# Batch 0's q turned once per pair, factors in the bank of the product of values, a fourth buffer of split P, and a new table of order

## The chip, the cores and the metric

The kernel runs on one core of a Trainium2 chip. The metric is the device time of one execution in microseconds (us); lower is better. An execution is timed as a whole; a profiled execution gives a trace of every instruction on the engines: TensorE (PE, matmuls; PEld its weight loads), VectorE (DVE), ScalarE (ACT), GpSimd (POOL) and SyncE (SP, which issues the DMAs).

## What is computed

Soft-capped attention over 4 batches, 12 heads, 448 positions and 64 columns per head, followed by two matrix products with a leaky relu between them. All inputs are fp32; cut to what matters:

```python
scores = q @ k.T / sqrt(64)                 # (4, 12, 448, 448)
scores = cap * tanh(scores / cap)           # cap = 30
attn   = softmax(scores, axis=-1)
x      = (attn @ v) -> (1792, 768)          # heads side by side
h      = x @ w_in                           # (768, 2048)
g      = max(h, 0) + alpha * min(h, 0)      # alpha per column
out    = g @ w_out                          # (2048, 768)
```

## The kernel before

Every step is put into one list, `Plan`, with a priority, the planner's guess of its time on each engine that may do it, and what it reads and writes. `order()` then plays the list through once on the host side, engine by engine, and the resulting order of each engine's queue is what the chip runs; nothing is reordered later. The guesses are constants at the head of the file: times of loads on SP (`load`, `load_w`, `LOAD_C`), `SWITCH` for a change of PE's tiling, `SAME` (how far down in priority PE may look for a step in the tiling that it is in), `PEN`, `PEN2` and `PENP` (what a step must gain before it goes to DVE or POOL). `OFF` adds a number to the priority of each group of steps. Where the plan has nothing ready for PE in the early part, it puts in fills: matmuls of the identity that compute nothing that is used (line 1236), one after another into a free bank.

PSUM is divided in two score tiles of two banks each (`s`) and four single banks (`p`). A step that needs a `p` bank takes a handle; of the kind that the attention uses at most three are out at once.

The work comes in three kinds. Attention goes by units, one pair of heads each. Batch 0 is done in exact fp32 in two parts, columns 0 to 192 of all six pairs (part 0), then 192 to 448 (part 1): `attention32` turns k (in part 0 only) and q by matmuls with the identity (`turn`, line 546; two fp32 matmuls for each of four chunks of 112 rows) and an eviction; then come scores (line 582), tanh, row maxima (line 623), exponentials (line 630), turns of P (line 734), and in `PV_32` the factors (1 over the row sums, spread along the columns by matmuls with the identity, line 796) and the product of values (line 807). The turned q of one part lies in one of two small buffers in `qkTs`, so each pair's q is turned once for each part: the chunks that the part touches, 2 of 4 in part 0 (4 matmuls) and 3 of 4 in part 1 (6 matmuls). The factors take a bank of their own and are evicted to `xs` first; then the product takes a second bank, and `xout_32` multiplies it with the factors on DVE and splits the result into two f16 halves in `xring`. Batch 1 has exact scores, and its first two units use `PV_32` as well, with all 448 columns. The other units use f16 pairs (high and low half): `split` makes them, P passes through one of `PW` buffers `pws` and is turned by a DMA (`ptall<-pw`).

The weights come as 64-bit words of which DVE makes fp32 (three steps, lines 1061, 1065 and 1071), and each is scaled and split into two f16 halves. The product with w_in (line 965) is evicted through the leaky relu (line 975) into `gall`; the product with w_out (line 1006) is evicted in halves of 384 columns (line 435) and stored by SP (line 1029).

In the program's names a digit behind a tile is a buffer: `wp6` and `wp7` hold the raw q of batch 0 (pairs 0 to 2 and 3 to 5), `wp4` and `wp5` its raw k, `wp0` to `wp3` the words of w_in; `rvs`, `nat`, `xring` and `vs16` take v of batch 0. `gall`, `tall` and `ptall` are lent to batch 0 for scores, turned k and turned P.

Of the kernel before, what the change touches and what calls it, by code (L numbers as in the profile page):

```python
# [31 lines left out]
B0_P = 174.12
LD_P = -270.26
LO_P = 908.9
MM_P = 2448.92
X_P = 475.19
ST_P = 63.05
ST1_P = -43.26
PV_P = 390.15
QK_P = -78.75  # L40
V_P = 196.4
WI_P = 21.53
WI_S = -63.55
A_S = 5.03
MM1_P = 480.9
WO_P = -182.63
WO_S = 86.83
WT_P = -1018.45
WT_S = 131.8
B1_P = 701.09  # L50
B_S = 239.81
EVAC_P = -930.96
# [13 lines left out]
PW = 3  # L66
QA = 0
# [5 lines left out]
SAME = 209.56  # L73
LOAD_C = (600, 1400, 950)
# [205 lines left out]
def kernel(  # L280
# [1003 lines left out]
```

## Time and profile before

| | |
|---|---|
| time, median of 3 runs | 671.75 us (669.79 to 672.01) |
| profiled execution, own time | 671.53 us |
| its span | 669.7 us |
| PE busy | 652.8 us (97%) |
| DVE busy | 466.5 us (70%) |
| ACT busy | 419.8 us (63%) |
| POOL busy | 264.1 us (39%) |
| chain that ended last | PE 78%, DVE 9%, ACT 6%, DMA 5% |

The busy time of an engine is summed over the whole span; a stretch in which two engines take turns, and one in which PE alone never stops, look alike in it. So the table is to be read with the row of tenths for each engine (40 slices of 16.7 us) and with tables by stretch. The first 140 us hold batch 0's and the start of batch 1's attention and the conversion of the weights; the last 400 hold mostly the two products.

### The profile page before, as it was taken

Reading aid. Unit: us, or ns where it says so; the run is one execution under the profiler, and the core shown is the slowest. Engines: PE = TensorE matmul, PEld = TensorE weight load, DVE = VectorE, ACT = ScalarE, POOL = GpSimd, SP = SyncE. Lnnn points to the kernel's source line nnn. Section 1 sums busy time; section 2 is a strip of 40 time slices with the busy share of each in tenths; the row PEclk is TensorE's granted clock in tenths of the full one; section 3 lists DMA queues with packets and bytes.
Section 4 is the critical chain, followed back from the end, with each engine's and each line's share of the span. In section 5 each row is a group of like instructions: output and inputs, shape, how many; then the busy total and the mean of one; then the engine's idle time right before and its main releaser. Section 6 shows DMA issues by size and latency. Waiting matters only on the chain.

```text
span 669.7 us, 13360 instructions
## 1 busy us (share of the span) xinstructions
PE 652.8 (97%) x5042; PEld 409.5 (61%) x5042; DVE 466.5 (70%) x887; ACT 419.8 (63%) x865; POOL 264.1 (39%) x393
## 2 busy tenths in 40 slices
PE   9999999799999999999999999999999999999997
PEld 8877777678877565554555555545555555556664
DVE  3799999999999858888887778889983104440000
ACT  2868999889789867778666567767783113331000
POOL 1224556257776724577664344556540000000000
PEclk9999999999999999999999999999999999999999
DMA  9998573954844499976939899686645300000111
GB/s 237 267 269 262 165 203 95 257 157 108 182 80 102 80 178 191 180 138 115 163 73 197 167 201 208 124 166 127 122 89 102 73 25 0 1 1 0 37 35 23
DMA packets 190048, 87.06 MB, mean 130 GB/s; under 512 B 156256, under 2 KB 186272, under 8 KB 189984
## 3 DMA queue, kind: packets, MB, share of 16 engines
q1 hardware_dynamic: 189840, 86.22, 59.6%
q8 instruction: 39, 0.64, 0.4%
q14 instruction: 25, 0.20, 0.1%
q10 hardware_dynamic: 144, 0.00, 0.0%
HBM read 45.82 MB, written 5.51 MB: 77 GB/s over the span
## 4 chain that ended last, share of the span: by engine, by line
PE 78%; DVE 9%; ACT 6%; DMA 5%; issue 2%; POOL 0%; ACTq 0%; SPq 0%; DVEq 0%; POOLq 0%
PE p L1006 29%; PE p L965 26%; PE p L780 5%; DMA ptall<-pw 4%; PE s L588 4%; PE s L582 3%; PE p L807 3%; PE p L1236 2%; PE p L734 2%; DVE mxs L623 2%; PE p L546 2%; ACT tall L630 1%; DVE wp L1065 1%; DVE wp L1071 1%; DMA rvs<-in_v_dram 1%
## 5 line engine op out<-in xcount | busy, mean ns | idle before, releaser
L965 PE MATMUL p<-xring,wi 128*128 128x448 f16 (+2 forms) x1440 | 225.0, 315 | 0.8 <-DVE vam L398 0.7
L1006 PE MATMUL p<-wp,gall 128*128 128x384 f16 x1344 | 223.3, 326 | 0.0
L965 PEld LDWEIGHTS <-wi 128*128 128x128 f16 x1440 | 135.2, 98 | 85.6 <-issue 6.1
L1006 PEld LDWEIGHTS <-gall 128*128 128x128 f16 x1344 | 129.7, 98 | 89.0 <-issue 5.3
L630 ACT ACTIVATE tall<-tall,mxs 128x448 f32<-128x448 f32 x126 | 82.8, 659 | 19.9 <-POOL mxs L625 9.7
L975 DVE SCALAR_TENSOR_TENSOR gr<-p,ca_g,gr 128x448 f32<-128x448 f32 (+2 forms) x80 | 46.8, 586 | 50.9 <-ACT gr L435 50.2
L623 DVE TENSOR_REDUCE mxs<-tall 128x2 f32<-128x896 f32 x63 | 67.6, 1079 | 8.5 <-ACT tall L619 7.9
L625 POOL TENSOR_SCALAR mxs<-mxs,small 128x2 f32<-128x2 f32 x59 | 30.5, 517 | 68.7 <-DVE mxs L623 56.1
L442 POOL TENSOR_TENSOR pw<-tall,pw 128x448 f16<-128x448 f32 x41 | 46.4, 1133 | 18.8 <-ACT pw L429 13.2
L435 ACT ACTIVATE wp<-p,small 128x384 f32<-128x384 f32 x22 | 12.7, 577 | 63.5 <-PE p L1006 63.5
L435 ACT ACTIVATE gr<-p,cs_g 128x448 f32<-128x448 f32 (+2 forms) x55 | 30.3, 550 | 30.5 <-PE p L965 30.1
L649 POOL TENSOR_SCALAR rr<-sums 128x2 f32<-128x2 f32 (+2 forms) x70 | 22.6, 323 | 65.6 <-ACT tall L630 49.2
L619 ACT ACTIVATE tall<-s,ams 128x896 f32<-128x896 f32 x42 | 41.5, 997 | 6.9 <-DVE pw L442 2.5
L429 ACT ACTIVATE pw<-tall 128x448 f16<-128x448 f32 x51 | 28.9, 571 | 24.6 <-DMA ptall<-pw 22.0
L429 ACT ACTIVATE gall<-gr 128x384 f16<-128x384 f32 (+4 forms) x60 | 27.4, 463 | 23.3 <-DVE gr L975 23.1
L780 PE MATMUL p<-ptall,vs 112*64 112x448 f16 x384 | 40.5, 355 | 0.6 <-DMA ptall<-pw 0.6
L442 DVE TENSOR_TENSOR pw<-tall,pw 128x448 f16<-128x448 f32 x43 | 29.8, 692 | 14.0 <-ACT pw L429 12.0
L442 DVE TENSOR_TENSOR gall<-gr,gall 128x64 f16<-128x64 f32 (+4 forms) x66 | 32.9, 499 | 6.2 <-ACT gall L429 3.2
L442 POOL TENSOR_TENSOR gall<-gr,gall 128x256 f16<-128x256 f32 (+4 forms) x46 | 34.0, 742 | 5.6 <-ACT gall L429 3.5
L780 PEld LDWEIGHTS <-vs 112*64 112x64 f16 x384 | 21.0, 110 | 18.6 <-issue 5.4
L435 ACT ACTIVATE tall<-tall,rr 128x448 f32<-128x448 f32 x42 | 27.0, 660 | 8.3 <-DVE rr L652 7.3
L588 PE MATMUL s<-qkTs 64*128 64x448 f16 (+1 forms) x288 | 28.3, 352 | 0.7 <-ACT tall L619 0.7
(175 smaller groups left out, 976.9 us busy)
## 6 DMA issues: line engine op xcount, KB each, us to landing
wp<-in_moe_w_in_dram SPq DMA_DIRECT2D x16, 768.0 KB, 7.7
wp<-in_moe_w_out_dram SPq DMA_DIRECT2D x16, 768.0 KB, 5.9
rvs<-in_v_dram SPq DMA_DIRECT2D x38, 224.0 KB, 3.3
rqk<-in_q_dram SPq DMA_DIRECT2D x12, 224.0 KB, 3.0
rqk<-in_k_dram SPq DMA_DIRECT2D x12, 224.0 KB, 3.5
ptall<-pw SPq DMA_TRANSPOSE x128, 3.2
wp<-in_q_dram SPq DMA_DIRECT2D x6, 224.0 KB, 7.3
wp<-in_k_dram SPq DMA_DIRECT2D x6, 224.0 KB, 9.3
```

Of the source, the lines that this page charges most:

```text
L429: nc.scalar.activation(out=o, in_=i, func=AF.Copy)
L435: nc.scalar.activation(out=o, in_=i, func=AF.Copy, scale=s)
L442: (nc.gpsimd if e == "pool" else nc.vector).tensor_tensor(out=o, in0=a, in1=b, op=ALU.subtract)
L588: yield lambda z=z, w=w: nc.tensor.matmul(s[rows, x, :S], q[a, z * S + cols.start:z * S + cols.stop], q[a, w * S:(w + 1) * S], start=(z == ...
L619: op(pr, {"act": (152 if reg else 245) + 377 * 2}, lambda e: nc.scalar.activation(out=t, in_=s[:, :, :S].rearrange("p c (j k) -> p c j k", ...
L623: op(pr, {"dve": 136 + 469 * 2}, lambda e: nc.vector.tensor_reduce(out=mt, in_=t, axis=AX.XY, op=ALU.max), r=tr, w=[mr], port=False)
L625: op(pr, {"dve": 200, "pool": 265}, lambda e: (nc.gpsimd if e == "pool" else nc.vector).tensor_scalar(out=mt, in0=mt, scalar1=ncap, scalar ...
L630: nc.scalar.activation(out=t[:, x], in_=t[:, x], func=AF.Exp, scale=capr, bias=mt[:, x:x + 1], accum_out=sums[:, u.idx % 3, col + x:col + ...
L780: nc.tensor.matmul(pv[x * D:(x + 1) * D, :n], vs[:, z, c:c + D], u.pt[x][:CP, y * NCH + kc], start=(i == 0), stop=(i == len(prods) - 1))
L965: nc.tensor.matmul(ps_p[h.slot][:, :n], w[:, z, kk, :], x[:, d, o:o + n], start=(kk == 0 and z == d), stop=(kk == NPAIR - 1 and z == 1))
L975: op(pr, {"dve": 198 + 1.07 * n}, lambda e: nc.vector.scalar_tensor_tensor(out=t, in0=ps_p[h.slot][:, :n], scalar=ca_g[:, j:j + 1], in1=t, ...
L1006: nc.tensor.matmul(ps_p[h.slot][:, :NH], g[j][:, d, t * P:(t + 1) * P], w[:, z, hf * NH:(hf + 1) * NH], start=(j == 0 and z == d), stop=(j ...
```

## The change

Six things are changed. (1) The planner's constants and its table `OFF` are others, and the loads' times in the plan are shorter (w_in 3400 to 2350, w_out 2500 to 1950, q, k and v 1000 to 880 ns), which moves instructions on all engines. (2) Batch 0's q is turned once per pair, all four chunks in part 0, and the turned q is kept in the place of the raw one (`qT`, in `wp6` and `wp7`). (3) `PV_32` takes one bank instead of two: the product of values goes to columns 0 to n, then the factors to columns n to 2n of the same bank; `xout_32` evicts the factors, then multiplies. Since 2n must fit in 512 columns, batch 1's two units do 256 and 192 columns apart. (4) `PW` is 4 instead of 3. (5) `QA` is 1 instead of 0: the q and k of batches 2 and 3 are split by a scaling to f16 and two subtractions of 256 columns on DVE, instead of a scaling in fp32, a copy and a subtraction. (6) The very last eviction is cut in two halves of 192 columns, one on ACT and one on DVE, and the last store's second DMA is issued on ACT's queue.

The diff, with the two tables `OFF` (212 numbers each) and most of the constants left out:

```diff
-PEN = 11684.16
-PEN2 = -1614.45
-PENP = 10077.68
+PEN = 24324.02
+PEN2 = 429.82
+PENP = 13233.71
...
-PW = 3
-QA = 0
+PW = 4
+QA = 1.0
-SAME = 209.56
-LOAD_C = (600, 1400, 950)
+SAME = 531.89
+LOAD_C = (600, 1400, 800)
...
     qkTs = ct([P, 3, NQK, CP], F16, "qkTs")
-    aux = qkTs[:, 2].rearrange("p g t -> p (g t)").bitcast(F32)
-    qzs = [aux[:, i * 256:(i + 1) * 256] for i in range(2)]
-    qzr = [(("qkT", 2), i * 256, (i + 1) * 256) for i in range(2)]
     ident, identr = ct([P, P], F32, "ident"), ("ident", 0, 1)
     ones = ct([NF, P], BF16, "ones")
     mxt = ct([NF, 128], F32, "mxt")
-    xs = ct([P, 2, 2, 256], F32, "xs")
-    diags = xs.rearrange("p a b n -> p (a b n)").rearrange("p (i n) -> p i n", n=P)
-    xsf = xs.rearrange("p a b n -> p (a b n)")
+    xs = ct([P, 2, 256], F32, "xs")
     vs16 = ct([P, 2, 2, 2 * NCH * D], F16, "vs16")
...
     def load(prio, dst, src, b, pair, w):
-        op(prio, {"sp": (600, 1400, 1000)}, lambda e: nc.sync.dma_start(out=dst.rearrange("p (h c) -> p h c", h=2),
+        op(prio, {"sp": (600, 1400, 880)}, lambda e: nc.sync.dma_start(out=dst.rearrange("p (h c) -> p h c", h=2),
                                                           in_=heads(src, b, pair)), w=w)
     class Unit:
         pass
-    raw32, v0 = {}, {}
+    raw32, qT, v0 = {}, {}, {}
...
                 raw32[i, pair] = t, (("wp", i + pair // 3), o, o + n)
+                qT[pair] = wpair[i + pair // 3].rearrange("p a b -> p (a b)")[:, o:o + S]
                 plan.tag = 155 + 2 * pair + (i == 6)
...
-    def xs_parts(u, n):
-        o = 512 * (u.idx % 2) if n <= 256 else 0
-        return [(xsf[:, a:a + n], ("xs", a, a + n)) for a in (o, o + (256 if n <= 256 else 512))]
-
-    def PV_32(u, prio, n, vt, vr):
-        (R, rt), _ = xs_parts(u, n)
+    xs_no = [0]
+
+    def PV_32(u, prio, a, n, vt, vr):
+
         h = plan.handle("a")
-        def rows_of(e):
-            for i, c, y, rows, cols in u.facts:
-                nc.tensor.matmul(ps_p[h.slot][y * D:(y + 1) * D, cols], rr[:, i, c:c + 1].to_broadcast([P, D]), ident[:, rows], start=True, stop=True)
-
-        op(prio, {"pe": n / 0.6 + 65}, rows_of, r=[(("r", i), c, c + 1) for i, c, *_ in u.facts] + [identr], w=[h], mode=1)
-        op(prio, either(n, True, f=True), lambda e: scaled(e, R, ps_p[h.slot][:, :n], vb[u.b].s), r=[h, (vb[u.b].tok, 7, 9)], w=[rt], port=False)
-        g_ = plan.handle("a")
-
         def PV(e):
-            pv = ps_p[g_.slot]
+            ps = ps_p[h.slot]
             for kc in range(NCH):
                 for y in range(2):
                     c = (y * NCH + kc) * D
-                    nc.tensor.matmul(pv[y * D:(y + 1) * D, :n], vt[:, c:c + D], u.pv[y][:, kc],
+                    nc.tensor.matmul(ps[y * D:(y + 1) * D, :n], vt[:, c:c + D], u.pv[y][:, kc, a:a + n],
                                      start=(kc == 0), stop=(kc == NCH - 1))
-
-        op(prio, {"pe": 4 * (n / 0.6 + 20)}, PV, r=[("pt", z, z + 3 * u.js + n) for z in u.po] + [vr], w=[g_], rows=0.875, mode=1)
-        return g_
+            for i, c, y, rows, cols in u.facts:
+                if a <= cols.start < a + n:
+                    nc.tensor.matmul(ps[y * D:(y + 1) * D, n + cols.start - a:n + cols.stop - a], rr[:, i, c:c + 1].to_broadcast([P, D]),
+                                     ident[:, rows], start=True, stop=True)
+
+        op(prio, {"pe": 4 * (n / 0.6 + 20) + n / 0.6 + 65}, PV, w=[h], rows=0.9, mode=1,
+           r=[(("r", i), c, c + 1) for i, c, *_ in u.facts] + [identr, vr] + [("pt", z + a, z + a + 3 * u.js + n) for z in u.po])
+        return h
     def xout_32(u, prio, h, n, o):
-        x, ((R, rt), (t, tt)) = xring[:, xslot(u.b, u.pair)], xs_parts(u, n)
+        x = xring[:, xslot(u.b, u.pair)]
+        i = xs_no[0] % 2
+        xs_no[0] += 1
+        t, tt = xs[:, i, :n], ("xs", i, i + 1)
         hi, lo = x[:, 0, o:o + n], x[:, 1, o:o + n]
-        op(prio, {"dve": 160 + 1.04 * n}, lambda e: nc.vector.tensor_tensor(out=t, in0=ps_p[h.slot][:, :n], in1=R, op=ALU.mult),
-           r=[h, rt], w=[tt], port=False)
+        op(prio, either(n, True, f=True), lambda e: scaled(e, t, ps_p[h.slot][:, n:2 * n], vb[u.b].s), r=[h, (vb[u.b].tok, 7, 9)], w=[tt], port=False)
+        op(prio, {"dve": 160 + 1.04 * n}, lambda e: nc.vector.tensor_tensor(out=t, in0=ps_p[h.slot][:, :n], in1=t, op=ALU.mult),
+           r=[h], w=[tt], port=False)
         op(prio, either(n, pool=True), lambda e: copy(e, hi, t), r=[tt], w=[xr(u.b, u.pair, 0, o, n)])
...
             op(prio, either(S, True), lambda e, h=h: copy(e, kt[:, pair, :], ps_p[h.slot][:, :S]), r=[h], w=[ktr], port=False)
-        h = plan.handle("a")
         rq, rqr = raw32[6, pair]
-        c0 = o // CP
-        nch = -(-(o + n) // CP) - c0
-        qi = u.idx % 2
-        u.q, qr = qzs[qi][:, :n], (qzr[qi][0], qzr[qi][1], qzr[qi][1] + n)
-        op(prio, {"pe": 60 + 205 * nch}, lambda e, h=h: turn(h, rq, c0, nch), r=[rqr, identr], w=[h, qr], rows=0.7, mode=1)
-        op(prio, either(n, True), lambda e, h=h: copy(e, u.q, ps_p[h.slot][:, o - c0 * CP:o - c0 * CP + n]), r=[h], w=[qr], port=False)
-        u.k, u.qk, u.scores, u.scale, u.joint, u.dma = kt[:, pair], [qr, ktr], scores_32, [icap], [icap], False
+        if part == 0:
+            h = plan.handle("a")
+            op(prio, {"pe": 60 + 205 * NCH}, lambda e, h=h: turn(h, rq, 0, NCH), r=[rqr, identr], w=[h], rows=0.7, mode=1)
+            op(prio, either(S, True), lambda e, h=h: copy(e, qT[pair], ps_p[h.slot][:, :S]), r=[h], w=[rqr], port=False)
+        u.q = qT[pair][:, o:o + n]
+        u.k, u.qk, u.scores, u.scale, u.joint, u.dma = kt[:, pair], [rqr, ktr], scores_32, [icap], [icap], False
         po = u.idx % 2 * 8 * n
...
         def finish(u):
-            h = PV_32(u, u.prio + X_P, n, *v0[0, u.pair])
+            h = PV_32(u, u.prio + X_P, 0, n, *v0[0, u.pair])
             xout_32(u, u.prio + X_P, h, n, o)
...
         else:
-            h = PV_32(u, u.prio + PV_P, S, *u.v)
-            xout_32(u, u.prio + PV_P, h, S, 0)
+            for a, n in ((0, 2 * P), (2 * P, S - 2 * P)):
+                h = PV_32(u, u.prio + PV_P, a, n, *u.v)
+                xout_32(u, u.prio + PV_P, h, n, a)
...
         osc = vb[b].osc if t < 3 else joint[:, b // 2:b // 2 + 1]
-        op(EVAC_P + prio * 1e-4, either(NH, True, f=True), lambda e: scaled(e, osb[:, cols], ps_p[h.slot][:, :NH], osc),
-           r=[h, *oscs], w=[osr], port=False)
         last = b == B - 1 and t == 3
+        cut = 2 if last and hf else 1
+        for i in range(cut):
+            z = slice(i * NH // cut, (i + 1) * NH // cut)
+            times = {("act", "dve")[i]: either(NH // 2, True, f=True)[("act", "dve")[i]]} if cut > 1 else either(NH, True, f=True)
+            op(EVAC_P + prio * 1e-4, times, lambda e, z=z: scaled(e, osb[:, cols][:, z], ps_p[h.slot][:, z], osc),
+               r=[h, *oscs], w=[(osr[0], osr[1] + z.start, osr[1] + z.stop)], port=False)
         if hf == 0 and not last:
...
             for t0, m, dst in rows:
-                op(EVAC_P, {"sp": (550, 1000, 800)}, lambda e, p=p, m=m, dst=dst: nc.sync.dma_start(
+                queue = {"act": 60} if cut > 1 and p else {"sp": (550, 1000, 800)}
+                op(EVAC_P, queue, lambda e, p=p, m=m, dst=dst: (nc.scalar if e == "act" else nc.sync).dma_start(
                     out=dst[:, a], in_=osb[p:p + m, a]), r=[osr])
...
             t = flat
-        op(prio, {"sp": (550, 1800, (3400 if split else 2500) if wide else 1700)}, lambda e: nc.sync.dma_start(
+        op(prio, {"sp": (550, 1800, (2350 if split else 1950) if wide else 1700)}, lambda e: nc.sync.dma_start(
             out=t.rearrange("p (c f) -> p c f", c=DM // P) if split else t, in_=src), w=[(("wp", i), 0, 2 * DM)] if wide else [fr])
```

Where instructions stand in the two programs is shown at two places. On SP, the first loads of the program, before; `in_q`, `in_k` and `in_v` are 224 KB for one pair, `in_moe_w_in` is a chunk of 768 KB:

```order
L462 DMA wp6_99<-in_q_dram 112x2x256
L462 DMA wp4_97<-in_k_dram 112x2x256 x2
L1049 DMA wp0_93<-in_moe_w_in_dram 128x6x256
L462 DMA wp6_99<-in_q_dram 112x2x256
L462 DMA wp7_100<-in_q_dram 112x2x256
L1049 DMA wp2_95<-in_moe_w_in_dram 128x6x256
L462 DMA rvs_111<-in_v_dram 112x2x256 x2
L462 DMA wp4_97<-in_k_dram 112x2x256
```

and after, where the same lines have the numbers 457 and 1047:

```order
L457 DMA wp6_99<-in_q_dram 112x2x256
L457 DMA wp4_97<-in_k_dram 112x2x256 x2
L1047 DMA wp0_93<-in_moe_w_in_dram 128x6x256
L457 DMA wp6_99<-in_q_dram 112x2x256
L457 DMA wp7_100<-in_q_dram 112x2x256
L457 DMA wp5_98<-in_k_dram 112x2x256
L457 DMA nat_113<-in_v_dram 112x2x256
L457 DMA xring_109<-in_v_dram 112x2x256
L457 DMA wp4_97<-in_k_dram 112x2x256
L1047 DMA wp2_95<-in_moe_w_in_dram 128x6x256
```

Up to the fifth load nothing moves; then two loads of k and two of v stand ahead of the second chunk of w_in, which was sixth.

On PE, the first products of values of batch 0's part 0 (line 807 before, 792 after) with the factors (796 in both) around them, before; line 415 and 418 are the two halves of a maximum over partitions, line 734 is a turn of P:

```order
L796 MATMUL p_64<-ident,rr 64x128 x2
L796 MATMUL p_64<-ident,rr 64x64 x2
L415 MATMUL p_63<-ident,n_wi 4x128
L807 MATMUL p_65<-ptall,rvs 64x192 x8
L418 LDWEIGHTS ones
L418 MATMUL p_63<-mxt,ones 128x4
L796 MATMUL p_64<-ident,rr 64x128 x2
L796 MATMUL p_64<-ident,rr 64x64 x2
L734 MATMUL p_65<-ident,gall 112x128 x4
```

and after, where line 410 and 413 are that maximum and line 542 is a turn of q (`wp_100` is the raw q of pairs 3 to 5):

```order
L542 MATMUL p_63<-ident,wp_100 64x112 x8
L410 MATMUL p_65<-ident,n_wi 4x128
L792 MATMUL p_66<-ptall,rvs 64x192 x8
L796 MATMUL p_66<-ident,rr 64x128 x2
L796 MATMUL p_66<-ident,rr 64x64 x2
L413 LDWEIGHTS ones
L413 MATMUL p_65<-mxt,ones 128x4
L542 MATMUL p_63<-ident,wp_100 64x112 x8
```

The factors, which stood in a bank of their own (`p_64`) on both sides of other work, follow the product of values in its bank (`p_66`), and whole turns of q (8 matmuls) stand beside them.

## Rows read from the trace of the kernel before

**Rows 1.** The page, parts 1 and 2: busy time, and tenths of 40 slices

```profile
PE 652.8 (97%) x5042; PEld 409.5 (61%) x5042; DVE 466.5 (70%) x887; ACT 419.8 (63%) x865; POOL 264.1 (39%) x393
...
PE   9999999799999999999999999999999999999997
...
DVE  3799999999999858888887778889983104440000
```

**Rows 2.** Four stretches: length, then busy PE, PEld, DVE, ACT, POOL, clock, DMA

```profile
0.00:20.00 20.00, 18.55 (x258) 16.64 (x258) 8.38 (x15) 8.16 (x16) 3.54 (x13) 1.00 0.96 247
20.00:140.00 120.00, 110.47 (x1199) 86.85 (x1196) 114.89 (x209) 104.75 (x237) 48.23 (x73) 1.00 0.74 207
140.00:265.00 125.00, 123.60 (x1050) 90.13 (x1048) 108.72 (x201) 102.73 (x214) 79.33 (x101) 1.00 0.68 137
265.00:665.00 400.00, 399.94 (x2542) 215.91 (x2541) 234.48 (x463) 203.53 (x400) 133.02 (x208) 1.00 0.52 100
```

**Rows 3.** Chain of waits in order of time: start, us, engine, tile, line, count

```profile
1.46 3.59 PE p L1236 x32
5.05 3.12 PE p L546 x40
8.17 3.23 PE p L1236 x56
...
12.66 1.71 PE s L582 x16
...
19.22 0.92 PE p L546 x16
...
38.24 1.45 PE p L807 x16
...
103.13 1.73 PE p L807 x16
...
136.63 3.23 PE p L807 x16
...
226.78 2.06 PE p L1006 x12
...
344.64 13.76 PE p L1006 x84
```

**Rows 4.** Waits of PE, 20 to 140 us: sum in us, times, longest

```profile
PE p L734 <- ACT ptall L429: 4.4, 5, 1.1
PE p L904 <- ACT ptall L429: 0.9, 1, 0.9
```

**Rows 5.** Evictions by line and shape: busy us, mean ns, then idle before

```profile
L429 ACT ACTIVATE tall<-p 128x448 f32<-128x448 f32 x4 | 2.2, 538 | 1.7 <-PE p L546 1.7
L435 ACT ACTIVATE xs<-p,vam 128x256 f32<-128x256 f32 x5 | 2.4, 475 | 0.0
L435 ACT ACTIVATE xs<-p,vam 128x192 f32<-128x192 f32 x5 | 2.0, 417 | 2.0 <-DVE xs L817 1.7 <-PE p L796 0.2
L429 ACT ACTIVATE qkTs<-p 128x192 f32<-128x192 f32 x5 | 1.6, 326 | 6.7 <-PE p L546 6.7
L429 ACT ACTIVATE qkTs<-p 128x256 f32<-128x256 f32 x4 | 1.4, 380 | 0.0
```

**Rows 6.** Timeline of the last microseconds: start, us, engine, line, operation

```profile
663.97 3.07 SPq L1029 DMA_DIRECT2D out_dram<-wp  x4
665.32 0.58 ACT L435 ACTIVATE wp<-p,joint 128x384 f32<-128x384 f32 x1 [1.38 <-PE p L1006]
```

**Rows 7.** Landings of loads issued at 2.7 (q), 4.0 (w_in) and 4.8 (v)

```profile
DMA to landing us min/median/max: 7.1/7.1/7.1
...
DMA to landing us min/median/max: 9.2/9.2/9.2
...
DMA to landing us min/median/max: 9.3/9.3/9.3
```

**Rows 8.** Timeline of DVE: second chunk's first step; a factor eviction

```profile
15.62 0.55 DVE L1061 TENSOR_SCALAR wi<-wp 128x768 int32<-128x768 int32 x1
...
36.73 0.42 DVE L439 TENSOR_SCALAR xs<-p,vam 128x192 f32<-128x192 f32 x1
```

More of the change, by code (lines that the diff above doesn't have):

```diff
@@ L28 @@
 AQ = 3
-PEN = 11684.16
-PEN2 = -1614.45
-PENP = 10077.68
[L32 to L52, printed above, removed]
+PEN = 24324.02
+PEN2 = 429.82
+PENP = 13233.71
+B0_P = 250.67
+LD_P = -207.13
+LO_P = 1890.42
+MM_P = 6687.03
+X_P = 667.61
+ST_P = 117.78
+ST1_P = -42.95
+PV_P = 180.1
+QK_P = -338.71
+V_P = 252.08
+WI_P = -374.93
+WI_S = -48.3
+A_S = 13.82
+MM1_P = 493.59
+WO_P = -142.86
+WO_S = 62.91
+WT_P = -1745.7
+WT_S = 152.86
+B1_P = 620.29
+B_S = 132.46
+EVAC_P = -1002.09
 LAT = 35.0
@@ L82 @@
 EXPONENT = 0x7F800000
-OFF = [-272.1, 0.0, 1.6, -199.0, 72.3, -342.5, -164.9, -398.1, -589.3, -18.8, -215.9, -279.5, 38.2, -373.9, -677.2, -465.3, 0.0, -4.4, -88.5, -0.9, -428.1, -154.8, -63.9, -608.1, -2526.1, 196.5, -1720.9, -249.2, 23.1, 15.0, -103.1, 154.2, 151.3, 146.8, -340.8, -418.8, -82.9, -32.3, 12.4, -158.2, 0.0, 34.6, 0.3, -13.2, 154.8, 771.7, -361.0, 53.8, -217.7, 41.8, -55.5, -42.5, 0.0, 49.5, 253.5, -526.8, 270.9, 64.6, -197.6, -107.1, 143.1, 973.6, -97.7, -369.5, -283.7, 440.1, -119.1, -88.2, -38.3, -67.3, -40.2, 270.9, -5204.2, -3719.4, -684.7, -4860.9, -3425.2, 690.8, -4676.0, 87.5, -600.9, -212.7, -3801.1, 567.9, -4121.8, -622.7, 281.5, 1.2, -930.1, -585.4, 71.5, 146.6, 167.3, 198.9, 122.3, -2317.2, -1028.1, -28.3, 134.4, 32.9, -382.2, 175.8, -24.2, -72.8, -2067.5, 7.4, -1382.8, 74.9, 0.5, -61.6, 83.9, 14.7, 85.1, -5.0, -6.8, 27.7, 86.0, 693.0, 565.8, -284.7, 6.1, 103.9, 35.0, -20.6, -34.6, -150.3, -2594.5, -5745.9, -3843.3, -5635.6, -6584.4, -3679.8, -6400.9, -6856.7, -2039.3, -7342.2, 0.0, -600.6, -637.3, -113.8, -6981.7, 0.0, 60.4, 305.4, 344.2, 169.7, 238.7, 679.0, -530.1, 154.6, -598.9, 947.6, 252.5, 392.1, 655.1, -8832.9, -10116.0, -9234.8, -3523.6, -2949.7, -2918.2, -2827.4, -3084.9, -2536.6, 25.0, -2289.5, -20.1, -3223.0, -3295.1, -2551.8, -2778.9, -2460.9, -2837.4, -320.8, 1520.7, -443.0, 392.6, 2071.1, 1996.9, -4256.5, -2575.0, -2757.3, -1733.7, -980.3, -485.7, -98.0, -1243.5, -806.6, -711.2, -794.2, -726.6, -711.2, -566.9, -533.0, 12.8, 850.2, 4312.8, 3340.9, 1497.3, 4244.7, 875.1, 535.6, 1281.8, 4692.8, 664.6, 9174.3, 1942.5, 5658.1, 2381.7, 1597.9, 5932.2, -436.2]
@@ new lines @@
+OFF = [3.2, -401.1, 51.6, -139.2, 1454.6, 45.4, 49.8, -38.2, -674.3, -24.9, 39.6, 25.1, 158.3, -197.5, -914.5, -88.5, 509.5, -178.6, 60.3, 0.0, -1155.4, -66.4, -213.9, -817.7, 80.9, 223.2, -262.7, 162.2, -263.5, -63.5, -48.8, 49.8, -256.2, 272.2, -674.8, -1321.6, 1531.5, 161.9, 273.3, 23.0, 228.0, 224.1, 138.3, 162.3, -70.6, 30.6, -8.0, -59.3, 30.1, -251.0, -100.4, 5.5, -69.7, 0.0, 190.4, 1595.1, -152.2, 194.8, -431.9, -189.3, -1491.2, -862.4, 160.4, -1336.1, 33.2, -298.2, 425.3, -180.6, 0.0, 254.3, -23.0, -3.7, 263.9, -37.4, -38.9, -2097.2, -19.9, -1.4, -1522.5, -29.8, 647.0, -1770.0, 0.0, 0.0, -2980.8, 103.4, 1914.1, -557.4, 537.1, 33.2, 0.0, -723.6, -373.5, 666.0, 575.6, -2208.6, 45.7, 308.9, -17.0, 277.2, -3.3, -236.9, -75.7, -356.6, -424.1, -182.7, -3431.1, 182.9, 247.3, 272.4, 199.8, 432.4, 188.3, 97.9, 326.3, -20.1, 35.8, 424.1, -507.3, -84.4, -664.4, -36.3, -30.7, 155.2, -3774.1, -4705.4, -2233.8, -2244.6, -3489.6, -1814.7, -1501.8, -3152.5, -2525.4, -6577.6, -3901.4, -7294.4, -6281.6, -5181.6, -5400.1, -5863.8, -9408.1, -4749.4, 31.4, -11.9, 122.6, -3734.2, -450.2, 1153.7, -124.3, -50.9, -94.9, 6155.4, 2068.9, -169.5, -343.4, -8404.7, -9228.1, -8931.4, -5436.4, -4226.4, -3789.6, -4921.0, -5305.1, -3359.5, -409.5, -2852.4, 56.1, -4291.1, -4249.4, -2856.7, -4858.0, -4928.0, -3627.5, -1585.6, -3201.7, -1945.6, -301.3, -781.1, 155.4, -5983.9, -3358.0, -3814.4, -282.7, 13.0, 89.7, 103.9, -3.1, 445.1, -30.9, -43.1, -148.3, -92.7, -159.7, -48.8, 183.8, -1697.3, -20.0, -2624.2, -1773.8, -5.0, -2469.5, 7.9, -2409.3, -2334.6, -16.3, -17.6, -2663.0, -2434.4, -2901.0, -2971.5, -2452.3, -655.0]
@@ L559 @@
     both = pt32[:CP, :16 * nA].rearrange("p (i j h t) -> p i j h t", i=2, j=NCH, h=2)
-    xpos = {}
     def xslot(b, pair):
```

## Prediction

> **What bounds the kernel now.** I read the page's parts 1 and 2 first, then one table of four stretches, then the chain of waits, and only then single lines. The page puts TensorE (PE) at 97% of the span; its row of tenths is full except for one slice, the eighth, while VectorE (DVE) is at 7 to 9 tenths over the same first half [rows 1]. The four stretches say what the average hides [rows 2]. From 265 to 665 us PE is busy 399.94 of 400 us: a wait on any other engine there costs nothing, and only work taken off PE counts. From 140 to 265 it loses 1.4 us. From 20 to 140 it loses 9.5 of 120 us, while DVE is busy 114.9. In the first 20 it loses 1.45 us, all of it the start (PE's first instruction stands at 1.46 [rows 3]). Between 20 and 140 the two engines are about equally loaded; PE's waits there are for evictions of its transposes by ScalarE (ACT), the largest sum being 4.4 us in 5 waits [rows 4], and those evictions stand behind what DVE must deliver. So before 140 us the bound is shared, and DVE's chain matters as much as PE's work; behind 140 the bound is PE alone.
>
> The profiled run took 671.53 us with a span of 669.7, thus 1.8 us outside it; the median of the three runs is 671.75. I make the sum against 671.53 and let the 0.2 us between them go.
>
> **The change part by part.** First, what goes from PE, counted in the two orders (how many instructions stand there) and priced from rows.
>
> Fills: 222 before, 175 after, thus 47 fewer. 32 early ones took 3.59 us (112 ns each), 56 later ones 3.23 us (58 ns) [rows 3]. In both orders about 31 stand at the very start, so those that go are of the cheap kind: 47 x 58 ns = 2.7 us.
>
> Turns of batch 0's q: each pair's q took 4 matmuls in part 0 and 6 in part 1 and now takes 8 once. That is 12 instructions fewer over six pairs; the trace has two records for each fp32 one, and 16 records take 0.92 us [rows 3], 57.5 ns each: 24 x 57.5 = 1.4 us. Six evictions go with them, mostly on ACT: 192 and 256 columns cost 326 and 380 ns, one of 448 costs 538 [rows 5], so 6 x (326 + 380 - 538) = 1.0 us less eviction work in all. That is off PE.
>
> Changes of tiling on PE (full array, row pairs, column pairs): 180 before, 154 after. By the place, 108 become 77 ahead of the first product with w_out, and 72 become 76 behind it; my 27 fewer are those two differences (the one instruction at the boundary makes no odds). The price of one: a stretch of 84 products with w_out in a row takes 13.76 us, that is 1.966 for 12, and 12 that stand alone between other work take 2.06 [rows 3]: 94 ns. 27 x 94 = 2.5 us. Here the larger reach in priority (SAME) and the factors put behind the product of values (one stretch of column pairs instead of two, as the second order piece shows) do the work.
>
> The product of values itself keeps its columns. Only batch 1's two exact units change, 448 into 256 + 192: 3.23 against 1.73 + 1.45 us [rows 3], nothing. Sum on PE: 2.7 + 1.4 + 2.5 = 6.6 us.
>
> The end: the last eviction, 384 columns on ACT, takes 0.58 us, and the four output DMAs of the last tile have been issued by 667.04 (663.97 + 3.07) [rows 6]. The last two are issued after the eviction's end at 665.90, 0.57 us each. A second issue on ACT's queue, beside SP's, saves 0.57. The two halves read one bank, and among the waits that the changed program lists DVE's half waits for ACT's, and both stores for DVE's. So they go one after the other: 417 ns for 192 columns on ACT [rows 5], 0.42 on DVE [rows 8], 0.84 and a hand-over of some 0.05, thus 0.31 more than now. The end gains 0.57 - 0.31 = 0.26 us.
>
> The Trainium skill, "PSUM — Partial Sum Buffer", section "PSUM bank collisions raise a hardware error", speaks against this edit: two engines must not touch one bank in the same partitions at once, though they only read different columns. No run here shows such a collision; by that rule the halves could not be freed from each other, and without it the sum would gain 0.57 + 0.16 = 0.73 there instead of 0.26.
>
> The factors in the product's bank: the eviction of factors (475 ns for 256 columns [rows 5]) used to run beside the product, in another bank. Now one bank holds both, and the eviction, the multiply and the release of the bank come after it. In the trace PE has no wait on these tiles among its larger ones [rows 4], so x of a pair is not what PE waits for next; by the rows the price is nothing. Its upper bound is 16 such evictions laid fully into the path, 16 x 0.48 = 7.6 us, less likely since other units' scores and transposes stand between.
>
> The fourth buffer for split P and the direct splits of batches 2 and 3 (three passes become a scaling and two half-width subtractions on DVE): all lies in stretches where PE is busy 123.6 of 125 and 399.94 of 400 us [rows 2], covered by the products with w_in and w_out. I put both at nothing; if the cover is gone, the 1.4 us that PE loses between 140 and 265 is what they could give, or take. DVE's work, each instruction at its row's mean, falls from 466.6 to 457.0 us.
>
> The order: two things could cost. The first SP piece shows four loads of 224 KB (two k, two v) ahead of w_in's second chunk. That chunk, issued at 4.0, landed 9.2 later, at 13.2, and a 224 KB load issued at 4.84 landed 9.3 later, at 14.1 [rows 7]: 0.87 us for one, so the chunk comes at 13.2 + 4 x 0.87 = 16.7. DVE took it up at 15.62 [rows 8]: up to 1.1 us of DVE's idle time. And with 53 fills instead of 99 ahead of the first scores PE reaches the turn of pair 1's q earlier than its data: three turns after 31 fills (3.5 + 3.4 us, as the first 40 records took 3.12) end near 8.2, 22 fills end near 9.5; that q, issued at 2.7, lands 7.1 later, at 9.8 [rows 7]: 0.3 us. In between lie smaller shifts that no row prices. I take +1.6 us for all waits: 1.1 + 0.3 and a little for the rest. Bounds: -1.5 (DVE gets its first work earlier by the loads that moved up) to +7 (next part).
>
> Why the rest may be kept although DVE is busy too: adding row means along both orders, the last point before the full stretch where PE waits on DVE stands behind 131.8 us of DVE work and 133.3 of PE work before, and behind 137.4 and 139.0 after. DVE's lead is the same 1.5 us, but what PE has left behind that point falls from 652.8 - 133.3 = 519.5 to 646.2 - 139.0 = 507.2. That is 12.3 less behind, against 5.6 more ahead: 6.7, the same as PE's own sum. More products with w_in now stand ahead of that point. Sum: -6.6 - 0.26 + 1.6 = -5.3, and 671.53 - 5.3 = 666.2 us.
>
> **The rivals.** A, the waits take it back: 31 of the changes of tiling that go, all turns and nearly all fills stand before 140 us, where DVE is busy 114.9 of 120 us [rows 2]. In the new order DVE's lead over PE is thin over a longer way (3 to 5 us at 80 to 125 us of PE work, where it was 8 to 10), so PE may simply wait where it used to fill. Then only the tail's 0.26 us and something of the moved products remain: about 670.5, from 669 to 673. Against it: the same count of 1.5 us at the last point.
>
> B, the slower side: PE's clock falls back in the opening. Granted clock reads 1.00 in every stretch [rows 2], yet the first fills go at 112 ns and those behind 8 us at 58 [rows 3], half the pace, which is the lower of the two levels, 1.2 GHz, after an idle start. If the shorter run of fills lets it stay or fall there between 7 and 20 us, five turns (0.92), two sets of scores (1.71) and the transposes, some 10 us of work, take twice as long: +10, of which some 1.5 lies in waits. 666.2 + 8.5 = 674.7. It decides where a pause of PE lets the clock go; the 0.3 us gap that I expect is less than the 1.46 us at the start, against it. The Trainium skill, "TensorE: Matmul & The Clock Gate", section "HAM oscillation — how this bites in real kernels", tells of pauses for data that make the next burst start cold; no wait of this trace shows it behind 8 us.
>
> C, better: transfers for q of pairs 4 and 5 and for w_out come earlier and DVE starts its conversions sooner, so that of the 9.5 us that PE loses between 20 and 140 [rows 2] about half goes: 666.2 - 5 = 661.2.
>
> **How the numbers follow.** The forecast (gain of 3 to 9 us, 662.5 to 668.5) has 0.60, A 0.22, C 0.12, B 0.06. A measurement of this kernel tells 0.3% from no change, 2.0 us: faster is below 669.7, slower above 673.8. Of A, 0.04 falls to faster, 0.13 to same, 0.05 to slower. Faster: 0.60 + 0.12 + 0.04 = 0.76; same 0.13; slower 0.05 + 0.06 = 0.11. The range 661.5 to 672.0 leaves out B, A's upper end and the better part of C.
>
> **What would show it.** In the profile after: PE busy about 646 us; fills about 12.8 us in 175; PE idle before 140 us about 11 to 13 us, with waits of PE on ACT's evictions as now; from 265 on as full as now; the span's end 0.26 us closer to the last product, with DVE's half of the last eviction behind ACT's. PE idle of 16 us or more before 140 would be A; fills or turns behind 8 us at twice 58 ns would be B; PE idle under 8 us would be C. I am wrong in the steady stretch if PE shows more than 2 us of waits behind 265 us, on split P or on the direct splits.

## The result: slower by 0.7%, and where the time went

The changed kernel takes 676.31 us (median of 12 runs) against 671.52 before (12 runs); the ratio is 1.0073, 95% interval 1.0049 to 1.0096. The forecast was 666.2 us. The profiled execution took 677.45 us with a span of 675.7; the line of its page that answers to [rows 1]:

```profile
PE 648.9 (96%) x5003; PEld 410.0 (61%) x5003; DVE 460.8 (68%) x886; ACT 418.3 (62%) x868; POOL 269.3 (40%) x395
```

PE does less, 648.9 us instead of 652.8, and the span is 6.0 us longer, so its idle time grew from 16.9 to 26.8 us. The four stretches of [rows 2], after (same columns):

```profile
0.00:20.00 20.00, 15.81 (x226) 13.43 (x228) 6.86 (x14) 8.49 (x14) 1.94 (x13) 1.00 0.96 233
20.00:140.00 120.00, 108.66 (x1192) 90.38 (x1190) 109.33 (x199) 100.30 (x224) 55.10 (x74) 0.99 0.74 208
140.00:265.00 125.00, 121.49 (x1036) 88.65 (x1033) 110.24 (x197) 103.39 (x225) 79.66 (x104) 1.00 0.65 131
265.00:665.00 400.00, 396.68 (x2521) 213.96 (x2521) 233.99 (x478) 205.07 (x407) 132.60 (x204) 1.00 0.53 102
```

Idle time of PE in them: 4.2 (before 1.45), 11.3 (9.5), 3.5 (1.4) and 3.3 us (0.06). No stretch kept its cover, and the last one, which I had called full, lost 3.3 us. The waits of PE by what ended them (sum in us, times, longest), after:

```profile
PE p L542 <- DMA wp<-in_q_dram: 3.0, 3, 1.3
PE p L896 <- DMA rqk<-in_q_dram: 2.4, 1, 2.4
PE p L729 <- ACT ptall L424: 2.2, 5, 0.6
PE p L775 <- DMA ptall<-pw: 1.8, 4, 0.7
...
PE p L775 <- issue: 1.3, 1, 1.3
```

The waits for evictions [rows 4] fell from 4.4 to 2.2 us. Those for the loads of q are new (line 542 turns batch 0's q, line 896 batch 1's), and those of line 775, the split product of values, for its turned P have grown (line 780 before: 0.6 us). Here are the pieces of PE's timeline around two of these loads (start, us, idle time before it and what ended it):

```profile
7.62 1.40 PE L1234 MATMUL p<-ident 128*128 128x128 f16 x22
10.37 1.84 PE L542 MATMUL p<-ident,wp 112*64 112x112 f32 x32 [1.35 <-DMA wp<-in_q_dram]
...
45.71 0.28 PE L1234 MATMUL p<-ident 128*128 128x128 f16 x2
48.42 0.57 PE L896 MATMUL p<-ident,rqk 112*128 112x112 f32 x4 [2.44 <-DMA rqk<-in_q_dram]
48.93 3.14 PE L577 MATMUL s<-tall,wp 64*128 64x224 f32 x16
...
54.66 1.78 PE L577 MATMUL s<-tall,wp 64*128 64x224 f32 x16
```

The 16 score matmuls at 48.93 take 3.14 us, 16 of the same shape at 54.66 take 1.78. Between them the granted clock (last column but two) fell to half, right behind the pause:

```profile
46.00:48.00 2.00, 0.00 (x0) 0.00 (x0) 2.00 (x3) 1.73 (x6) 1.80 (x3) 1.00 1.07 317
48.00:50.00 2.00, 1.58 (x12) 1.41 (x14) 2.00 (x4) 0.56 (x2) 0.97 (x1) 0.80 1.09 345
50.00:52.00 2.00, 2.00 (x13) 1.38 (x9) 1.34 (x2) 0.92 (x1) 0.00 (x0) 0.50 1.15 279
52.00:54.00 2.00, 2.00 (x25) 1.78 (x25) 0.94 (x2) 1.90 (x4) 0.00 (x0) 0.85 1.20 286
```

That is some 3.4 us at the lower of the two levels (1.2 GHz), 1.7 us of work lost. Every run lists the mean granted clock of its execution: over 11 executions of the changed kernel (the twelfth, 949.5 us at a clock of 0.655 throughout, is left out) it is 0.9963 on average, over 29 of the kernel before 0.9989. Of 672 us that is 2.5 against 0.7 us, so by this estimate 1.8 of the 4.8 us are the clock's. A straight line through the times of the changed kernel's 23 executions (these and the 12 of the next run) is in line with it: 0.6 us for each 0.001 of clock, and 673.7 us at full clock.

### The profile page after: what moved, and what is told of

Its sections match the earlier page's. It is cut to its first block, busy times and chain, and to the rows that moved or that the text cites. A ratio compares the mean times of both kernels' runs of the same rounds, so it can differ in the third digit from the quotient of the medians.

```text
span 675.7 us, 13258 instructions
## 1 busy us (share of the span) xinstructions
PE 648.9 (96%) x5003; PEld 410.0 (61%) x5003; DVE 460.8 (68%) x886; ACT 418.3 (62%) x868; POOL 269.3 (40%) x395
## 5 line engine op out<-in xcount | busy, mean ns | idle before, releaser
L620 POOL TENSOR_SCALAR mxs<-mxs,small 128x2 f32<-128x2 f32 x68 | 38.7, 570 | 60.3 <-DVE mxs L618 52.7
L437 POOL TENSOR_TENSOR pw<-tall,pw 128x448 f16<-128x448 f32 x47 | 52.5, 1123 | 21.8 <-ACT pw L424 20.5
L430 ACT ACTIVATE gr<-p,cs_g 128x448 f32<-128x448 f32 (+2 forms) x63 | 35.1, 556 | 39.5 <-PE p L958 37.3
L437 POOL TENSOR_TENSOR gall<-gr,gall 128x192 f16<-128x192 f32 (+4 forms) x52 | 43.9, 848 | 15.8 <-ACT gall L424 11.3
L644 POOL TENSOR_SCALAR rr<-sums 128x2 f32<-128x2 f32 (+2 forms) x70 | 25.1, 360 | 57.0 <-ACT tall L625 35.0
L437 DVE TENSOR_TENSOR pw<-tall,pw 128x448 f16<-128x448 f32 x37 | 24.5, 665 | 14.9 <-ACT pw L424 13.6
L437 DVE TENSOR_TENSOR gall<-gr,gall 128x64 f16<-128x64 f32 (+4 forms) x60 | 27.5, 464 | 6.9 <-ACT gall L424 4.4
L432 POOL TENSOR_SCALAR tall<-tall,rr 128x448 f32<-128x448 f32 x32 | 25.3, 792 | 13.5 <-DVE rr L647 12.5
```

What stands on the lines that cost most here:

```text
L430: nc.scalar.activation(out=o, in_=i, func=AF.Copy, scale=s)
L432: nc.gpsimd.tensor_scalar(out=o, in0=i, scalar1=s, scalar2=1.0, op0=ALU.mult, op1=ALU.mult)
L437: (nc.gpsimd if e == "pool" else nc.vector).tensor_tensor(out=o, in0=a, in1=b, op=ALU.subtract)
L620: op(pr, {"dve": 200, "pool": 265}, lambda e: (nc.gpsimd if e == "pool" else nc.vector).tensor_scalar(out=mt, in0=mt, scalar1=ncap, scalar ...
```

## The experiments

Most of them keep the changed kernel's planned order and move or add a few steps in it; the kernel before ran beside each. Four ran on one chip first.

**The changed kernel again.**

> The changed kernel once more, on the chip of the runs beside it: near 676.3 us as its median was. In its profile the turn of batch 1's first q waited 2.44 us for its load at 46 us, and behind that pause the granted clock fell to half for 3.4 us. If both belong to the order, they show again; if the clock's fall is chance, this profile may lack it, and the time is then nearer to 674.

Measured: 675.88 us against 672.0 before, ratio 1.0066 (1.0040 to 1.0091). Its profile has two falls of the clock, at other places (21 and 103 us), and none at 49, though PE waits 1.72 us for the same load there. So the place is not fixed; that this order has falls is.

**Batch 1's first q ahead of two chunks of w_out.** What the edit does to SP's queue:

```diff
-DMA wp<-in_moe_w_out
 DMA wp<-in_moe_w_in
-DMA rqk<-in_q (one half)
-DMA wp<-in_moe_w_out
-DMA rqk<-in_q (the other half)
+DMA rqk<-in_q x2
+DMA wp<-in_moe_w_out x2
```

> The changed kernel with one edit on SP's queue: the two chunks of w_out that stand between the last q of batch 0 and batch 1's first q go behind that q (the planned order is otherwise kept on every engine). Theory L (the late load costs what it shows): PE has its q at about 41 us instead of 48.3, the pause of 2.44 us and the half clock (3.4 us, thus 1.7 lost) go, 4.1 us less: 672 us. Rival D (DVE and ACT set the pace up to 200 us): the pause goes, but other waits take its place before 140 us, and only the clock's 1.7 us or less come back: 674.5 to 676.

Measured: 673.7 us, ratio 1.0034 (1.0012 to 1.0057): 2.2 us less than the changed kernel beside it. The pause is gone; the turn (line 906 in this kernel) follows the fills with no wait, and the scores take 1.78 us:

```profile
46.03 0.28 PE L1244 MATMUL p<-ident 128*128 128x128 f16 x2
46.14 0.56 PE L906 MATMUL p<-ident,rqk 112*128 112x112 f32 x4
46.62 1.78 PE L587 MATMUL s<-tall,wp 64*128 64x224 f32 x16
```

Half of the 4.1 us came back, between the two theories. The mean clock rose from 0.9953 to 0.9978, by the count above 1.7 of the 2.2 us; so the pause itself seems to have cost little. Falls of the clock still come (the 0.9978 stand for 1.5 us).

**42 fills in that pause.**

```diff
+        t = min(i for i, x in enumerate(steps) if name(x) and name(x)[0] == "turn_c")
+        f = max(i for i in range(t) if name(steps[i]) == "fill")
+        steps[f + 1:f + 1] = [steps[f]] * 42
```

> The changed kernel with 42 more fills (2.4 us of matmuls that compute nothing) put before the turn of batch 1's first q; the load stays late. Theory L: PE is no longer idle in the pause, the clock stays at full, 1.7 us come back: 674.6. Rival D: the lost 1.7 us were covered by DVE's work anyway, no difference: 676.3. If the clock falls although PE is busy, the pause was not its cause.

Measured: 674.63 us, ratio 1.0029 (1.0005 to 1.0053), 1.3 us less than the changed kernel beside it. The q is as late as before, PE is busy, and the clock stays full there:

```profile
44.00:48.00 4.00, 4.00 (x58) 3.40 (x57) 4.00 (x6) 3.34 (x6) 1.04 (x2) 1.00 1.07 316
48.00:52.00 4.00, 3.83 (x50) 3.27 (x48) 4.00 (x6) 2.48 (x6) 2.06 (x3) 1.00 1.12 327
```

That the clock stays full there proves little: in four other traces with that late load (the changed kernel again, and three runs below) the same load leaves a pause of 1.72 to 2.29 us and no fall follows. So it is in the kernel with the end in one piece:

```profile
48.34 0.58 PE L896 MATMUL p<-ident,rqk 112*128 112x112 f32 x4 [2.15 <-DMA rqk<-in_q_dram]
48.84 1.78 PE L577 MATMUL s<-tall,wp 64*128 64x224 f32 x16
```

Work that computes nothing seems to have made the kernel faster, if by little. In its profile one fall stands elsewhere, near 230 us, behind a pause of 1.82 us. The differences of these three on one chip are of the size of their intervals (0.5% wide), so the ordering is likely, not certain.

**The kernel before with 32 of its 222 fills.**

```diff
+        fills = [i for i, x in enumerate(steps) if name(x) == "fill"]
+        drop = set(fills[32:])
+        steps = [x for i, x in enumerate(steps) if i not in drop]
```

> The kernel before, its order kept, with only the first 32 of its 222 fills; 190 are taken out (they compute nothing). The prediction's step (a fill costs 58 ns of PE's time): 190 x 58 = 11 us less, 661. Rival W (fills stand where PE would wait for data anyway): the same 672, PE's idle time before 140 us grows by about 11 us. With the clock in it: pauses in place of fills let the granted clock fall to half more often, 1.7 us for each fall, so 673 to 677.

Measured: 671.17 us against 671.45, ratio 0.9998 (0.9977 to 1.0018). Taking out 11 us of PE's work changed nothing at the median, but the 12 executions fall in two groups: six with a granted clock of 0.997 to 1.000 take 668.8 to 669.8 us, six with 0.987 to 0.989 take 672.5 to 674.4. Against 671.45 the three with 1.000 (669.0 on average) are 2.4 us faster: at full clock a fill costs some 13 ns and not 58; and without them the mean clock is over 1% down in half of the executions. The profile (one of the first group) shows the waits that took their place, and a granted clock of 0.83 behind them:

```profile
10.96 0.60 PE L556 MATMUL p<-ident,wp 112*64 112x112 f32 x8 [2.88 <-DMA wp<-in_q_dram]
11.50 2.72 PE L592 MATMUL s<-tall,qkTs 64*128 64x224 f32 x14
...
10.00:20.00 10.00, 8.02 (x85) 5.92 (x86) 8.29 (x10) 5.84 (x14) 2.30 (x3) 0.83 1.13 248
```

**The kernel before without its 74 late fills**, and the last store's second DMA on ACT's queue (beside the lines above):

```diff
+        drop = set(fills[148:])
+                queue = {"act": 60} if last and hf and p else {"sp": (550, 1000, 800)}
```

> The kernel before with two edits: the 74 fills behind 20 us are left out (4.3 us of matmuls that compute nothing; the 148 ahead of that stay), and the second DMA of the last store goes on ACT's queue, with the eviction in one piece. By the run with 32 fills a fill in a wait costs nearly nothing (190 of them 2 us at full clock), so the 74 give at most 0.8; the store gives 0.4. With the opening's fills kept, the granted clock should stay at full as in the kernel before: 670.5. If the later fills were what keeps the clock, its falls come back and the time is 672 or more.

Measured: 672.59 us against 672.07, ratio 1.0008 (0.9989 to 1.0027). The mean granted clock is 0.9955, in the kernel before beside it 0.9988: the late fills, too, were holding it. A miss for my 670.5; the second branch of the expectation came.

**The end in one piece.**

```diff
-        cut = 2 if last and hf else 1
+        cut = 1
```

> The changed kernel with its last eviction in one piece on ACT again, the last store's second DMA still on ACT's queue. From the end of PE's last product to the end of the span the kernel before takes 4.48 us, the changed one 4.4. Theory: the halves run one behind the other (0.43 + 0.42 us in the trace after), one piece takes 0.58, so 0.3 us less than the cut: 4.1. If the halves had run side by side, 0.15 more than the cut.

The ends of the two timelines, after and then uncut:

```profile
671.40 0.42 ACT L430 ACTIVATE wp<-p,joint 128x192 f32<-128x192 f32 x1 [1.38 <-PE p L999]
671.85 0.42 DVE L434 TENSOR_SCALAR wp<-p,joint 128x192 f32<-128x192 f32 x1 [60.35 <-ACT wp L430]
672.30 0.53 ACTq L1027 DMA_DIRECT2D out_dram<-wp  x1
```

```profile
667.38 0.58 ACT L430 ACTIVATE wp<-p,joint 128x384 f32<-128x384 f32 x1 [1.38 <-PE p L999]
667.99 0.53 ACTq L1027 DMA_DIRECT2D out_dram<-wp  x1
```

DVE's half begins when ACT's has ended. From the last eviction's start to the end of the span it is 4.38 us before (665.32 to 669.7), 4.30 after (671.40 to 675.7), 4.02 uncut (667.38 to 671.4): the change's end gains 0.08, the second queue alone 0.36. This kernel's profile happens to have no fall of the clock, so it is also the clean trace of the changed order. It took 673.19 us (median of 5, ratio 1.0033, 1.0016 to 1.0051). Of its distance to the changed kernel's 676 us on other chips the end explains 0.3 us by the traces; the rest isn't taken apart.

**Reading the clean trace.** How many products stand on either side of 208 us (where the kernel before starts with w_out) and of 600 us tells which order is ahead. Rows: stretch, PE busy (count), clock, DMA share and GB/s. The product with w_out has not begun by 208 us before; in the uncut kernel (line 999):

```profile
0.00:208.00 208.00, 4.26 (x26) 1.00 0.69 184
```

Both have done the same 576 products with w_in and the same attention by then. The changed order is 26 products, 4.3 us, ahead at 208 us. All of PE, then the fills alone (lines 1236 and 1234), before:

```profile
0.00:208.00 208.00, 196.46 (x2112) 1.00 0.71 186
0.00:208.00 208.00, 16.26 (x222) 1.00 0.71 186
```

and uncut:

```profile
0.00:208.00 208.00, 193.22 (x2097) 1.00 0.69 184
0.00:208.00 208.00, 13.26 (x173) 1.00 0.69 184
```

Without fills and w_out PE's own work is 180.2 us before and 175.7 uncut, 4.5 less. Fills and idle time together are 27.8 and 28.0: what the fills gave up, waits took. So the lead is PE's own work. Then the product with w_in behind 600 us, before (line 965) and uncut (line 958), each with 384 of w_out still to do:

```profile
600.00:676.00 76.00, 2.83 (x15) 0.98 0.08 21
```

```profile
600.00:676.00 76.00, 4.89 (x26) 0.99 0.08 21
```

It is 11 products of 0.19 us, 2.1 us, behind. Between 208 and 600 us, where I had put nothing, it loses 6.4 us. All of PE in that stretch, before first, then uncut:

```profile
208.00:600.00 392.00, 391.10 (x2535) 1.00 0.63 119
```

```profile
208.00:600.00 392.00, 386.65 (x2500) 1.00 0.64 120
```

Its idle time grew from 0.9 to 5.4 us, and the same work keeps PE busy 1.9 us longer, for which no run gives the reason. The waits, before first, then uncut:

```profile
PE s L588 <- ACT tall L619: 0.7, 1, 0.7
PE p L780 <- DMA ptall<-pw: 0.2, 1, 0.2
```

```profile
PE p L775 <- DMA ptall<-pw: 1.9, 3, 0.7
PE p L413 <- DVE mxt L408: 0.8, 1, 0.8
PE p L775 <- issue: 0.7, 1, 0.7
PE p L410 <- DVE vam L529: 0.6, 1, 0.6
PE p L999 <- DVE gr L968: 0.6, 1, 0.6
PE p L410 <- DVE ams L379: 0.4, 1, 0.4
```

**Four of those products of values later.** Products with w_in or w_out, whose inputs are there, go ahead of them:

```diff
-PV_split(unit), mm
+mm, PV_split(unit)
```

> The changed kernel with one or two products with w_in or w_out (about 2 us each) put ahead of four of the split products of values that stalled on their P in the trace after (the second, fourth, tenth and twelfth such product); this time each moved product has everything it reads ready at its new place, which the five moves of pv_late did not keep (its time is therefore no measure). Theory P (PE alone counts behind 208 us, and it stalls there on P): the stalls inside those products fall from 4.6 us to about 1.5: 673. Rival S (the stalls move on): 676.

Measured: 679.03 us, ratio 1.0110 (1.0081 to 1.0138), some 3 us slower than the changed kernel on other chips. The four stalls are gone (another such product waits 0.9 us in their place), but PE's waits behind 208 us sum to 8.6 us, the four largest:

```profile
PE s L610 <- ACT tall L641: 2.6, 4, 1.1
PE p L440 <- DVE mxt L435: 2.0, 1, 2.0
PE p L437 <- DVE small L420: 1.8, 2, 1.4
PE p L802 <- DMA ptall<-pw: 1.1, 2, 0.9
```

The products moved forward had been the cover of other steps: a score waits for its tile, a maximum (line 440) for DVE. Rival S, and more than it said. An earlier form (pv_late, 687.1 us, and the same with the q's load moved, 686.8) put the products of values behind steps that they have to precede; those two are no measure.

**All three together.**

```diff
-DMA wp4<-in_moe_w_out, DMA wp5<-in_moe_w_out, DMA rqk<-in_q
+DMA rqk<-in_q, DMA wp4<-in_moe_w_out, DMA wp5<-in_moe_w_out
-PV_split(unit), mm
+mm, PV_split(unit)
-        cut = 2 if last and hf else 1
+        cut = 1
```

> The changed kernel with three edits: batch 1's first q ahead of the two chunks of w_out (alone: 675.9 to 673.7), the four moves of pv_late2, and the last eviction in one piece (0.3 us in the trace). If they add up: 676 - 2.2 - 2.5 - 0.3 = 671, at or a little under the kernel before (671.5 to 672.0); in executions without a fall of the granted clock 669. If the moves gain nothing: 673.5.

Measured: 679.73 us, ratio 1.0119 (1.0092 to 1.0147). The moves' loss decides; beside it the q's load and the end show no gain.

**Which edit makes P late?** Three mixtures of code and table:

```diff
-QA = 1.0
+QA = 0
```

> The changed kernel with the splits of batches 2 and 3 in three passes again (scaling, copy, subtraction); PE's order is the same up to about 240 us, and the number of fills too. Theory O (the new order, not the direct split, lets PE run into P and scores that are not ready behind 208 us): the stalls inside the split products of values stay near 4 us and the time near 676. Rival Q (the two subtractions on DVE per split make P late): the stalls fall to about 1.5 us and the time to 673.

Measured: 676.2 us against 671.01, ratio 1.0069 (1.0042 to 1.0096). Line 775 still waits (behind 208 us, qa0):

```profile
PE p L413 <- DVE mxt L408: 3.8, 3, 3.0
PE p L775 <- DMA ptall<-pw: 1.9, 3, 0.7
PE p L775 <- issue: 0.4, 1, 0.4
```

With the three passes back the time is the same, so the direct split alone is not the cause; as PE's order differs behind some 240 us, what it does to single waits isn't shown. The fourth buffer of P wasn't tried alone.

The new code under the old table (first lines of the edit; the other constants and the rest of the table are left out):

```diff
-SAME = 531.89
+SAME = 209.56
-        op(prio, {"sp": (600, 1400, 880)}, ...
+        op(prio, {"sp": (600, 1400, 1000)}, ...
...
-OFF = [3.2, -401.1, 51.6, ...
+OFF = [-272.1, 0.0, 1.6, ...
```

> The changed code (q turned once, factors in the product's bank, four buffers, direct splits, the cut end) under the planner's constants, load times and table of the kernel before. Theory T (the new order loses, the code does not): at or below the kernel before, 668 to 672. Rival K (the code's edits lose, for instance by the factors' eviction behind the product or by more work on DVE in the splits): 674 or more. The old table was not made for this code, so up to 2 us above before would still be no proof for K; the profile's waits decide.

Measured: 696.83 us (4 runs), ratio 1.0367. Its plan puts in 572 fills, 305 of them between 140 and 265 us: the table leaves holes for this code. The split products wait 0.3 us for P.

The old code under the new table (cut in the same way):

```diff
-SAME = 209.56
+SAME = 531.89
-        op(prio, {"sp": (600, 1400, 1000)}, ...
+        op(prio, {"sp": (600, 1400, 880)}, ...
...
-OFF = [-272.1, 0.0, 1.6, ...
+OFF = [3.2, -401.1, 51.6, ...
```

> The code of the kernel before under the new constants, load times and table (three buffers and three-pass splits as before); its plan holds 208 fills. Theory O (the order is the cause): more than 3 us of stalls inside the split products of values, as in the kernel after, and a time of 674 or more. Rival Q or the other edits of the code: stalls near 1.5 us as in the kernel before, and at most 672. The table was not made for this code, so the time alone decides nothing; where PE waits does.

Measured: 700.77 us (4 runs), ratio 1.0448, and a mean granted clock of 0.978: between 20 and 60 us PE is busy 24.8 of 40 us. Its split products wait only 0.7 us for P. Against theory O as far as it goes: the table alone does not bring those waits. Both are misses for me: a table made for one list of steps says little on the other. That the waits come from the order in which code and table together put products of values is what is left, and argued; which step of the pair is not shown.

## Why the prediction was wrong, step by step

**What bounds the kernel.** That PE alone counts behind 140 us was right. The step that failed is the next one: "all lies in stretches where PE is busy 123.6 of 125 and 399.94 of 400 us [rows 2], covered by the products". The rows showed that the old order had no waits there, not that the stretch has slack. In the new order PE waits there mostly for steps of the attention's chain (scores, softmax, split, P's transposes, product of values), and 6.4 us went that I had priced at nothing: 4.5 of idle time and 1.9 of longer work. This alone is more than the forecast's gain. I had named the sign (more than 2 us of waits behind 265 us on split P; line 775 has 2.5 there in the profile after) but given it no chance. Why the chain comes late in this order stays open.

**Fills.** 47 x 58 ns = 2.7 us was mis-sized: the run with 32 fills has them at 13 ns, 0.6 us for 47, and in the clean trace the idle time took back all that they gave (27.8 against 28.0 us). In the opening PE waits for q instead: the turn at 10.37 us waits 1.35 us where 56 fills stood [rows 3], and the first scores start at 12.64 instead of 12.66 us.

**Turns and changes of tiling** weren't measured apart. In the sum they have 4.3 us ahead of 208 us (1.4, and 31 changes at 94 ns); in the clean trace PE's own work there is 4.5 us less, so this part was right. The fills' 2.7 less the 1.6 of waits were to add 1.1 and added nothing (-0.2).

**The order's cost.** I had priced two loads. The second chunk of w_in didn't show as a wait of PE. The first gate was 1.35 us instead of 0.3: q landed at 10.3 instead of 9.8, and PE came to it at 9.0. What I missed stands on the same queue further down: two chunks of w_out ahead of batch 1's first q, 2.44 us and a fall of the clock. I had counted the earlier w_out as a gain (rival C). Rival A, that waits ahead of 140 us take the gain back, has its mark nearly met: 15.5 us of idle time there in the profile after, where it named 16 and the forecast 11 to 13.

**Rival B** had the right mechanism at the wrong place and nearly five times too large (8.5 us): no long fall in the opening, but single falls of 3.4 us, in the first four traces of this order at five places between 21 and 230 us, by the estimate 1.8 us more of them than before on average. The Trainium skill, "TensorE: Matmul & The Clock Gate", section "HAM oscillation — how this bites in real kernels", describes that sequence, pause and then a cold burst; the pause of 2.44 us and the 0.50 behind it agree. The 2.15 us in the clean trace with 1.00 behind them do not.

**The end**: 0.26 forecast, 0.08 measured; the halves do go one behind the other.

In sum: -4.3 (by 208 us), +6.4 (208 to 600) and -0.1 (end) are +2.0 at full clock (by the straight line it is 673.7 us, and the executions of the kernel before at 0.999 or 1.000 beside the second run average 671.6), and with +1.8 (clock, estimated) +3.8, against 4.8 between the medians; the rest is within what the runs tell.

## What to carry to other kernels

An engine that is busy 399.94 of 400 us proves that its present order has no waits there, not that a new order will have none; a table of order is to be re-read for each queue, transfers first. Matmuls that fill a wait were nearly free here (13 ns each) and helped to hold TensorE's clock, so take a fill's price only where the engine would otherwise have had work. Where a chain through several engines runs beside the bound engine, moving one wait off it can show the next, as the four moved products did (8.6 us of waits).

## What the hardware showed

Falls of the granted clock came mostly singly, some 3.4 us each at half, and at other places in the two profiles of the changed kernel (49, then 21 and 103 us). The traces of both kernels and of ten runs (the old code under the new table and the two with wrong moves left out) hold ten. Seven came behind a pause of PE of 1.8 to 3.0 us, three (at 37, 101 and 103 us) behind a row of pauses of 0.2 to 0.8 us. But five pauses of 1.7 to 2.3 us had no fall behind them: in these traces a pause of that size was followed by a fall about as often as not. The spread of the run times (673.45 to 681.88 us for the changed kernel) follows the clock in part. The kernel before with its 222 fills has no fall in its profile, and 0.9989 on average.
